# Attention with experts: biases turned group by group behind the first scores, and logits with the values' weights stationary

## The chip, the cores and the metric

One core of a Trainium2 chip. TensorE (PE) multiplies, VectorE (DVE), ScalarE (ACT) and GpSimd (POOL) do elementwise work, SyncE issues most transfers. The metric is the device time of one launch in microseconds; the kernel before takes 784.1 us, the median of 3 runs (784.02 to 784.55). All arithmetic is in fp32. A layer named tile records the kernel's operations and adds the waits between engines; an engine works through its operations in the order in which the kernel names them.

## The reference

Attention over 8 batches of 8 heads, 576 positions, 64 channels, with a bias made of a running sum; its output, 512 channels per token, goes to one of 8 experts per token.

```
# attention, per batch and head
scores = q @ k.T / 8
cum    = cumsum(max(s, 0))                       # one number per position
bias   = min(-(cum[i] - cum[j]), 0)
attn   = softmax(where(j > i, -1e9, scores + bias))
x      = attn @ v                                # (B, S, H * D) after the heads are put side by side
# experts, per token
logits     = x @ w_gate                          # 8 numbers
local_gate = sigmoid(x @ w_local)                # 1 number
e   = argmax(logits) if first token or local_gate < 0.5 else the expert of the token before
out = softmax(logits)[e] * (relu(x @ w1[e]) @ w2[e])
```

## The kernel before

Two heads make a pair; there are 32 pairs (`NPAIR`). The 576 positions are four blocks of 128 keys (`NF`) and a tail of 64 (`TL`); queries stand in nine tops of 64. A pair's scores are computed key by key (keys in partitions) in three units, each in a two-bank PSUM buffer of a pool of three; ScalarE makes weights of them with `exp(scale * score + bias)`, where the bias is one number per key, relative to the middle of one of two groups of queries (`GROUPS`). So the running sum has to be turned once, at the start, from heads in partitions to keys in partitions:

```
spin(18)                                          # 18 matmuls of the identity, results unused
nc.vector.tensor_scalar_max(s_sb, s_sb, 0.0)
cum = t_in.tile([BH, S], F32, name="cum")
nc.vector.tensor_tensor_scan(cum, ones, s_sb, 0.0, op0=Alu.mult, op1=Alu.add)

bps = ps_s.tile([P, 2, 512], F32, name="bps", tag="s")[:, 0]
bias_of, at = {}, 0
for g, (q0, q1) in enumerate(GROUPS):
    n = -(-q1 // P) * P if g == 0 else S
    rel = t_in.tile([BH, n], F32, name=f"rel{g}")
    nc.vector.tensor_scalar(rel, cum[:, :n], cum[:, MIDS[g] : MIDS[g] + 1], None, Alu.subtract)
    for c, a in enumerate(range(0, TS, P)):
        if a + P <= n:
            tr(bps[:, at : at + BH], rel[:, a : a + P], ident[:BH, :BH])      # 3 in group 0, 4 in group 1
            ...
for h in range(2):
    mm(bps[h * TL : h * TL + TL, at : at + NPAIR], lhsT=rel[:, TS:], rhs=ident[:BH, h:BH:2], start=True, stop=True)
...
nc.vector.tensor_copy(bias, bps[:, :at])
```

Two PSUM banks, `banks[0]` and `banks[1]`, take the rows: weights times values, for two sets of query tops. The values' tile holds, beside the values of both heads, a column of ones for the sums, and room for the token's logits: `v @ [w_gate, w_local]` is computed ahead and set beside `v`, so that the rows come out with the token's share of the logits. Before, the small weights are stationary in four column groups (32 columns each, 18 of them in use), the values stream, and the result is turned in VectorE:

```
scores_of_tail = banks[0][:, 3 * VW : 3 * VW + TL]                  # VW = 148
gates = banks[1][:, 2 * VW : 2 * VW + NB * SLOT].rearrange("p (c n) -> p c n", c=NB)   # SLOT = 32, NB = 5

def tail_scores(n):
    for h in range(2):
        d = slice(DH * h, DH * h + DH)
        mm(scores_of_tail[d], lhsT=ins[n][1][:, TS:][:, d], rhs=ins[n][0][:, TS:], start=True, stop=True)

def gate_parts(n):
    m = P // 4
    v = ins[n][2].rearrange("p (c n) -> p c n", c=NB)
    for j in range(0, P, m):
        mm(gates[j : j + m], lhsT=wz[:, n % HP], rhs=v[:, :, j : j + m], start=True, stop=True)

def beside_v(n):
    nc.vector.transpose(ins[n][3][:, :, 1 + DH : 1 + DH + SLOT], gates)
```

The rows of a pair, and the loop over pairs:

```
for h, d in enumerate(PARTS):                     # inside rows(n, g), for each query top i
    out = y[:, h * VW // 2 : (h + 1) * VW // 2]
    last = i * TL == TS
    if last:
        todo[half].append((out, scs[n, "tail"], v[:, NF, d], True, False))
    for c in cs:
        ...
        todo[half].append((out, scs[n, u][:, h, at : at + TL], v[:, c, d], not last and c == 0, c == cs[-1]))

tail_scores(0)
for n in range(NPAIR + 1):
    load(n + 3)
    if n < NPAIR:
        for u, pieces in enumerate((((0, 0), (3, 1)), ((0, 1), (1, 1)), ((2, 0), (2, 1), (1, 0)))):
            scores(n, u)
            for piece in pieces:
                weights(n, piece)
                if piece == (0, 0):
                    tail(n)                       # ScalarE reads the tail's scores
            ...
        seen_tail(n)
    ...                                           # steps of the sorting of tokens by expert
    if n:
        rows(n - 1, 1)
        divide(n - 1, 1)
        rows(n - 1, 0)
    else:
        spin(8)
    if n + 1 < NPAIR:
        tail_scores(n + 1)
    if n:
        divide(n - 1, 0)
    if n < NPAIR:
        gate_parts(n)
        beside_v(n)
    ...
```

In the experts' part, two of the gathered blocks of tokens are turned on PE (`product`, `x` is 128 tokens by their channels):

```
for c in range(DK):                               # DK = 4
    for h in range(2):
        self.nc.tensor.matmul(ps[h * DH : h * DH + DH, c, :], lhsT=rows[:, c, X0[h] : X0[h] + DH], rhs=self.ident,
                              start=True, stop=True)
```

## Time and profile before

| what | value |
|---|---|
| time, median of 3 runs | 784.1 us |
| span of the profiled execution | 782.4 us |
| VectorE, ScalarE, GpSimd busy | 43%, 30%, 23% |
| attention, first to last rows | 17.9 to 241.5 us |
| moved by transfers | 205.56 MB, 263 GB/s on average |

Line numbers (L406) are those of the kernel before. In a group of the profile, `o<-v,sc 128*64 128x74 f32 x3072` names the tiles written and read, the used rows and columns of the array (128 rows, 64 columns of weights), the streamed operand (128 partitions, 74 columns), and the number of records; an fp32 matmul leaves two records. Two numbers follow: busy time in us and the mean duration of one in ns, and then how long the engine was idle ahead of them. PE is the multiplying, PEld the loading of weights. Durations of records overlap, so the pace of PE is the distance between the starts of its records.

### The profile page before, as it was taken

The page shows a single profiled execution, that of the slowest core. Times are in us where ns is not written, and L with a number is a line of the kernel's source. Part 1 is how long each engine was busy: PE and PEld are TensorE (multiplying, and loading weights), DVE is VectorE, ACT ScalarE, POOL GpSimd, SP SyncE. Part 2 cuts the span into 40 slices and gives each one's busy share as a digit, 9 for nine tenths or more (in the row PEclk, how much of TensorE's full clock was granted, in tenths as well). Part 3 has the DMA queues.
Part 4 walks back from the last instruction along what each step waited for, and adds up shares of the span by engine and source line. Part 5 has one row for each costly group of instructions (what it writes and reads, how often), then busy time and mean ns, then how long its engine had stood idle before and what let it go on. Part 6 is the DMA issues. An engine that isn't in the chain of part 4 may idle for free.

```text
span 782.4 us, 17629 instructions
## 1 busy us (share of the span) xinstructions
PE 773.0 (99%) x6782; PEld 546.2 (70%) x6782; DVE 339.0 (43%) x1196; ACT 237.2 (30%) x611; POOL 176.2 (23%) x329
## 2 busy tenths in 40 slices
PE   9999999999999999999999999999999999999996
PEld 8888888888887846836677366773657736676762
DVE  2334444455566748315562156521565215635000
ACT  5777767776762111111111111111111111111110
POOL 4432345456450421011110111101111011011001
PEclk9999999999999999999999999999999999999999
DMA  9586679988655499966997569976699766994001
GB/s 314 187 300 194 201 244 327 326 285 262 210 208 217 131 354 390 409 228 221 376 395 297 199 224 380 392 290 208 233 365 389 297 211 228 368 409 175 10 13 44
DMA packets 64141, 205.56 MB, mean 263 GB/s; under 512 B 8269, under 2 KB 8301, under 8 KB 64048
## 3 DMA queue, kind: packets, MB, share of 16 engines
q1 hardware_dynamic: 55008, 173.55, 62.3%
q0 software_dynamic: 8896, 30.47, 10.4%
q8 instruction: 55, 0.90, 0.5%
q10 hardware_dynamic: 144, 0.33, 0.1%
q14 instruction: 38, 0.31, 0.1%
HBM read 181.08 MB, written 23.76 MB: 262 GB/s over the span
## 4 chain that ended last, share of the span: by engine, by line
issue 58%; PE 32%; POOL 5%; DVE 2%; POOLq 2%; DMA 1%; DVEq 0%
PE o L406 14%; PE ps L335 11%; POOL out_dram L1261 2%; POOL xg L1196 2%; PE hp L1243 2%; PE o L374 2%; PE o L291 1%; POOLq L1171 1%; DMA x_rows<-x,r_slot_i 1%; PE o L356 1%; PE bank L956 0%; DVE xT L1097 0%; POOL x_rows L1047 0%; PE bank L1107 0%; PE bank L981 0%
## 5 line engine op out<-in xcount | busy, mean ns | idle before, releaser
L1097 DVE STREAM_TRANSPOSE xT<-xg 32x128 f32<-32x128 f32 x576 | 174.1, 302 | 174.2 <-PE hp L1243 92.7
L1256 PE MATMUL yp<-w,hT 128*128 128x512 f32 (+1 forms) x528 | 216.4, 593 | 0.0
L1243 PE MATMUL hp<-xT,w 128*128 128x256 f32 (+1 forms) x1088 | 192.3, 337 | 0.3 <-DVE xT L1097 0.3
L1243 PEld LDWEIGHTS hp<-xT,w 128*128 128x128 f32 x1088 | 172.1, 191 | 24.6 <-issue 8.2
L344 ACT ACTIVATE sc<-ps,bias 128x256 f32<-128x256 f32 (+3 forms) x448 | 156.5, 482 | 53.6 <-PE ps L335 51.2
L1256 PEld LDWEIGHTS yp<-w,hT 128*128 128x128 f32 (+1 forms) x528 | 90.1, 180 | 114.6 <-issue 113.3
L1261 POOL DMA_INDIRECT out_dram<-y,at_gate x38 | 38.5, 1013 | 433.9 <-ACT y L1260 419.0
L406 PE MATMUL o<-v,sc 128*64 128x74 f32 x3072 | 113.6, 228 | 0.8 <-issue 0.8
L406 PEld LDWEIGHTS o<-v,sc 128*64 128x64 f32 x3072 | 108.8, 136 | 8.1 <-issue 4.3
L1247 ACT ACTIVATE hT<-hp 128x512 f32<-128x512 f32 x68 | 40.6, 597 | 193.0 <-PE hp L1243 193.0
L1260 ACT ACTIVATE y<-yp,at_gate 128x512 f32<-128x512 f32 x38 | 26.1, 687 | 239.8 <-PE yp L1256 233.6
L335 PE MATMUL ps<-q,k 64*128 64x320 f32 (+2 forms) x768 | 92.5, 386 | 0.1
L350 POOL TENSOR_SCALAR_AFFINE_SELECT sc<-sc 128x256 f32<-128x256 f32 x160 | 66.5, 420 | 115.9 <-issue 59.1
L335 PEld LDWEIGHTS ps<-q,k 64*128 64x128 f32 x768 | 68.9, 186 | 20.0 <-issue 4.8
L1256 PE MATMUL yp<-x,hT 128*128 128x512 f32 (+1 forms) x144 | 63.2, 594 | 0.0
L1234 DVE STREAM_TRANSPOSE hT<-x 32x256 f32<-32x256 f32 x64 | 27.9, 436 | 65.4 <-ACT x L1228 64.5
L1243 PEld LDWEIGHTS hp<-xT,x 128*128 128x128 f32 x320 | 46.1, 191 | 5.8 <-issue 2.6
L1243 PE MATMUL hp<-xT,x 128*128 128x128 f32 (+1 forms) x320 | 50.1, 317 | 0.0
L416 DVE RECIPROCAL recs<-o 128x4 f32<-128x4 f32 x64 | 12.1, 189 | 87.0 <-PE o L406 63.1
L1256 PEld LDWEIGHTS yp<-x,hT 128*128 128x128 f32 (+1 forms) x144 | 25.3, 178 | 26.2 <-issue 26.0
L1047 POOL DMA_INDIRECT x_rows<-x,r_slot_i x40 | 38.7, 968 | 10.1 <-issue 5.9
L419 DVE TENSOR_TENSOR x<-o,recs 128x292 f32<-128x292 f32 x64 | 34.4, 538 | 2.2
(162 smaller groups left out, 339.8 us busy)
## 6 DMA issues: line engine op xcount, KB each, us to landing
w<-in_w_dram SPq DMA_DIRECT2D x184, 512.0 KB, 9.5
x<-in_w_dram SPq DMA_DIRECT2D x56, 512.0 KB, 9.3
v<-in_vx_dram SPq DMA_DIRECT2D x32, 405.0 KB, 5.8
vt<-in_vz_dram SPq DMA_DIRECT2D x32, 320.0 KB, 3.9
k<-in_kz_dram SPq DMA_DIRECT2D x31, 320.0 KB, 5.1
q<-in_q_dram SPq DMA_DIRECT2D x32, 288.0 KB, 5.4
xg<-x_rows POOLq DMA_DIRECT2D x30, 293.0 KB, 8.5
x_rows<-r_empty SPq DMA_DIRECT2D x6, 293.0 KB, 3.6
```

The lines of the kernel that those rows point to most:

```text
L335: mm(ps[:, h, at : at + z - a], lhsT=kb[d, c * P : c * P + P], rhs=qb[d, a:z], start=True, stop=True)
L344: nc.scalar.activation(scs[n, u][:, h, at : at + z - a], raw[u][:, h, at : at + z - a], Act.Exp, bias=bias[:, i : i + 1], scale=scale)
L350: nc.gpsimd.affine_select(out=x, in_=x, compare_op=Alu.is_ge, fill=0.0, base=0, pattern=[[0, 2], [1, P]], channel_multiplier=-1)
L406: mm(y, lhsT=w, rhs=x, start=start, stop=stop)
L419: nc.vector.tensor_tensor(x, y, rec.unsqueeze(3).to_broadcast([P, t1 - t0, 2, HW]), op=Alu.mult)
L1047: self.s.nc.gpsimd.indirect_dma_start(out=next(self.s.views)[:, :], out_offset=bass.IndirectOffsetOnAxis(ap=self.slot[:z, m : m + 1], axis=0),
L1097: self.nc.vector.transpose(self.xT[i][d : d + m, :, k * P + a * m : k * P + a * m + m], rows[a * m : a * m + m, :, X0[d // DH] + d % DH :] ...
L1234: nc.vector.transpose(hT[i][d : d + m, :, a : a + m], x[a : a + m, :, d : d + m])
L1243: mm(y, lhsT=w[0][:, c, f : f + P], rhs=xT[i][:, c, :], start=(c == 0), stop=(c == DK - 1))
L1247: nc.scalar.activation(hT[i][:, g : g + per], ps, Act.Relu)
L1256: mm(ps[n * m : n * m + m, :], lhsT=hT[i][:, c, a : a + m], rhs=wn[:, c, :], start=(c == 0), stop=(c == FK - 1))
L1261: nc.gpsimd.indirect_dma_start(out=next(outs)[:, :], out_offset=bass.IndirectOffsetOnAxis(ap=at[i, k][:, 0:1], axis=0), in_=y[:, :], eleme ...
```

## The change

It has two parts. One is at the start: the spinning is shorter, the first pair's tail scores and two of its three score units come ahead of the biases' turning, the second group's subtraction is on GpSimd, and each group is turned into a bank of its own and copied by itself. The other takes back a layout: the values are stationary again in the logits' matmuls (64 columns at a time) and the small weights stream, so no turning in VectorE is needed, but two copies. With that the 18 columns need no slot of 32, a token's row is logits, values, values, logits, its 128 values lie side by side, the tail's rows of both heads are one matmul, the PE turning of tokens is a plain transpose, the tail's scores move to `banks[1]`, and each division follows its rows. The purpose of the first part is a shorter start, that of the second a simpler layout.

```diff
-SLOT = 32
-VX = 2 * DH + SLOT + 2
-PARTS = slice(0, VW // 2), slice(VX - VW // 2, VX)
-X0 = 0, 2 * HW - DH
+X0 = E + 1
...
-    scores_of_tail = banks[0][:, 3 * VW : 3 * VW + TL]
-    gates = banks[1][:, 2 * VW : 2 * VW + NB * SLOT].rearrange("p (c n) -> p c n", c=NB)
+    TAIL = 2 * VW
+    GATE = TAIL + TL
...
-    spin(18)
+    spin(11)
     nc.vector.tensor_scalar_max(s_sb, s_sb, 0.0)
     cum = t_in.tile([BH, S], F32, name="cum")
     nc.vector.tensor_tensor_scan(cum, ones, s_sb, 0.0, op0=Alu.mult, op1=Alu.add)
-    bps = ps_s.tile([P, 2, 512], F32, name="bps", tag="s")[:, 0]
+    bps = ps_s.tile([P, 2, 512], F32, name="bps", tag="s")
+
+    tail_scores(0)
+    for u in range(2):
+        scores(0, u)
...
-        nc.vector.tensor_scalar(rel, cum[:, :n], cum[:, MIDS[g] : MIDS[g] + 1], None, Alu.subtract)
+        (nc.gpsimd if g else nc.vector).tensor_scalar(rel, cum[:, :n], cum[:, MIDS[g] : MIDS[g] + 1], 1.0,
+                                                      Alu.subtract, Alu.mult)
...
-                tr(bps[:, at : at + BH], rel[:, a : a + P], ident[:BH, :BH])
+                tr(bps[:, g, width[g] : width[g] + BH], rel[:, a : a + P], ident[:BH, :BH])
...
-    nc.vector.tensor_copy(bias, bps[:, :at])
+    for g in range(2):
+        nc.vector.tensor_copy(bias[:, width[0] * g :][:, : width[g]], bps[:, g, : width[g]])
...
-            mm(scores_of_tail[d], lhsT=ins[n][1][:, TS:][:, d], rhs=ins[n][0][:, TS:], start=True, stop=True)
+            mm(banks[1][d, TAIL : TAIL + TL], lhsT=ins[n][1][:, TS:][:, d], rhs=ins[n][0][:, TS:], start=True, stop=True)
...
+    gates = banks[1][:, GATE : GATE + NB * 2 * (E + 1)].rearrange("p (c h e) -> p c h e", c=NB, h=2)
     def gate_parts(n):
-        m = P // 4
-        v = ins[n][2].rearrange("p (c n) -> p c n", c=NB)
-        for j in range(0, P, m):
-            mm(gates[j : j + m], lhsT=wz[:, n % HP], rhs=v[:, :, j : j + m], start=True, stop=True)
+        m = P // 2
+        for c in range(NB):
+            for j in range(0, P, m):
+                mm(gates[j : j + m, c], lhsT=ins[n][2][:, c * P + j : c * P + j + m], rhs=wz[:, n % HP],
+                   start=True, stop=True)
 
     def beside_v(n):
-        nc.vector.transpose(ins[n][3][:, :, 1 + DH : 1 + DH + SLOT], gates)
+        v = ins[n][3]
+        nc.vector.tensor_copy(v[:, :, 1 : E + 2], gates[:, :, 0])
+        nc.vector.tensor_copy(v[:, :, VW - E - 2 : VW - 1], gates[:, :, 1])
...
+                if last:
+                    todo[half].append((y, scs[n, "tail"], v[:, NF], True, False))
...
             rows(n - 1, 1)
-            divide(n - 1, 1)
             rows(n - 1, 0)
...                                                (the division now stands at the end of rows)
-                scores(n, u)
+                if n or u == 2:
+                    scores(n, u)
...
         for c in range(DK):
-            for h in range(2):
-                self.nc.tensor.matmul(ps[h * DH : h * DH + DH, c, :], lhsT=rows[:, c, X0[h] : X0[h] + DH], rhs=self.ident,
-                                      start=True, stop=True)
+            self.nc.tensor.transpose(ps[:, c, :], x[:, 2 * c * HW + X0 : 2 * c * HW + X0 + P], self.ident)
```

## Prediction

> **What bounds the kernel now.** I read the page first: busy shares, then the chain, then the groups of the lines that the change touches.

> ```profile
> PE 773.0 (99%) x6782; PEld 546.2 (70%) x6782; DVE 339.0 (43%) x1196; ACT 237.2 (30%) x611; POOL 176.2 (23%) x329
> ```

> PE is never idle for long; the other engines are under half busy. PE's busy time contains overlap, so I don't take it as a limit by itself, but the records leave only four holes above 80 ns: 1.55 us at the start, 0.13 us at 101, 0.84 us at 237 and 0.34 us at 241. So what PE gains or loses in its own order is gained or lost by the kernel, with one exception: at 237 PE waits for the last pair's weights.

> Next the chain in order of time, for its first 30 us (start, duration, what):

> ```profile
> 1.55 7.06 PE o L291 x36
> 8.62 0.58 PE bps L307 x7
> 9.19 0.23 PE bps L312 x4
> 9.43 0.27 PE o L356 x4
> 9.69 2.79 PE ps L335 x24
> 12.48 1.98 PE o L291 x16
> 14.46 0.27 PE o L356 x4
> 14.73 0.41 PE o L374 x8
> 15.14 2.79 PE ps L335 x24
> 17.93 3.42 PE o L406 x99
> ...
> 21.52 0.41 PE o L374 x8
> 21.93 2.79 PE ps L335 x24
> 24.72 3.42 PE o L406 x99
> ```

> The chain is PE alone. One pair of heads costs 24.72 - 17.93 = 6.79 us: scores (L335) 2.79, rows (L406) 3.4, tail scores (L356) 0.2, logits (L374) 0.41. There are 32 pairs. At the front stand 36 records (18 matmuls) of spinning, then the biases' turning, then the first scores.

> Third, the groups by shape:

> ```profile
> L406 PE MATMUL o<-v,sc 128*64 128x74 f32 x3072 | 113.6, 228 | 0.8 <-issue 0.8
> L406 PEld LDWEIGHTS o<-v,sc 128*64 128x64 f32 x3072 | 108.8, 136 | 8.1 <-issue 4.3 <-DVE tail L366 2.9 <-DVE r_code L944 0.5
> L374 PE MATMUL o<-vt,wz 128*32 128x160 f32 x256 | 15.7, 311 | 0.0
> L374 PEld LDWEIGHTS o<-vt,wz 128*32 128x32 f32 x256 | 5.1, 108 | 2.2
> ```

> Each fp32 matmul has two records: 256 are 4 matmuls for 32 pairs, 3072 are 48. A weight load takes 108 ns for 32 columns, 136 for 64, 191 for 128 (L1243): 0.87 ns per column on top of some 80 ns that overlap.

> [...] Two records in different column halves start 6 ns apart, and from the last tail-score pair (64 columns, halves) to the first logits record (quarters) pass 152 ns, where streaming 64 columns takes 56. So a change of mode costs about 96 ns. [...] my 0.87 ns per column gives 56. [...] Here spin records start every 213 ns up to 7.4 us and every 112 ns after.

> **The logits, 31 pairs that count** (the last pair's lie in front of the hole at 237).
> Before: from the first tail-score record to the next scores 21.12 to 21.86 = 0.74 us, with the switch from halves to quarters in it. Two passes of 160 columns: 0.16 us from the first to the second, 0.23 from there to the scores.
> After: 10 matmuls, 20 records, as 10 concurrent pairs (two halves), each with 64 columns of weights and only 18 to stream. They have the tiling of the rows and tail scores, so the first switch goes: the tail scores shrink from 0.33 to 0.23. What is the pace of a pair? In L406 it is 64 ns, where 74 columns at 0.83 to 0.84 ns (320 columns of L335 take 269) make 62: streaming bounds it, and two loads in parallel fit inside. With 18 columns streaming is 15 ns, so the load bounds: 56 plus a few, I choose 60. 9 x 60 = 0.54, then 0.015 for the last stream and 0.1 for the switch to the scores' 64 rows. Sum 0.23 + 0.54 + 0.115 = 0.89 us against 0.74: +0.155 per pair, x 31 = **+4.8 us**.

> **The tail's rows.** Two matmuls of 74 columns become one of 148: one load fewer, the same streaming, on the half of the array that was no shorter than the other. 0.

> **DVE.** One turning of 342 ns becomes two copies of 45 elements. The bias copy (480 elements 657 ns) and the reciprocal (4 elements 183) give about 1 ns per element: some 225 ns each, +0.1 us per pair. Their reader, the rows, comes 3 us later on PE: off the path.

> **A new tie through one PSUM bank.** Tail scores now lie in the bank of the first rows. In the program as built, the first rows matmul waits for ScalarE's tail weights of the next pair. In the trace before, that ScalarE instruction ends 0.40 us ahead of the rows' first record in most pairs (24.25 against 24.65), but only 0.00 to 0.14 ahead in eight of the 30, where the sorting work had kept ScalarE. Those eight may lose 0.05 to 0.1 each: **+0.5 us**. The tail scores now wait for VectorE's division of the first rows, which ends 0.265 us earlier in the first sixteen pairs: nothing.

> **The front.** Seven spins fewer: 22 records end at 6.40 instead of 36 at 8.5. The first q's last packet lands at 6.02, in time. Tail scores and two of the three score units cost 0.3 + 0.94 + 0.84 at full clock[...], +0.5: until 9.0. The turnings take 0.8 as before: last result at about 10.0 (SBUF subtraction on GpSimd is done by then; GpSimd is free from 6.6 us). Though the copies are split, in the built program the first of them waits for the last turning of the second group. So 10.05 + 0.3 + 0.45 = 10.8, and the third score unit, which needs the buffer of both, waits for both: PE stands for about 0.9 us. It runs 10.9 to 11.8, and the eight spins behind it start 0.6 us earlier than before (12.4). ScalarE starts 0.4 us earlier than its 10.86, which is worth nothing while PE leads. I take **-0.5 us**.

> **Two PE turnings of tokens** (L1107), 1.02 us each on the chain at 250.45 and 255.92, as eight matmuls of half width: 109 ns a pair. Now four full-width transposes with a single record each (those of the biases have one): 4 x 0.11, and no switch from and to the experts' full tiling, 2 x 0.1. About 0.5 saved each: **-1.0 us**.

> Sum: 4.8 + 0.5 - 0.5 - 1.0 = +3.8; 784.1 + 3.8 = **787.9 us**.

> **Rivals.**
> (a) The loads of two halves don't run in parallel when streaming no longer hides them: 2 x 56 = 112 ns a pair, +0.62 us per pair, +19 us in all: 803, slower by 2.4%. Against it: L406 sustains 64 ns a pair with the same loads. A floor of 79 ns, which two records of 2 columns in the sort (L981) show, would make +0.33 per pair: 793.
> (b) The pace falls to 50 or less, and the removed switch pays for the extra matmuls: +0.06 per pair, 785.
> (c) The tie through the bank acts in every pair: ScalarE's tail becomes the end of the wait, some 0.3 us each: 797. Against it: 0.40 us of room in 22 of 30 pairs[...].
> (d) The front gains more, because ScalarE led rather than PE: up to 2 us less, 786. Against it: the chain shows no ScalarE there, and ScalarE's wait of 8 us ended with PE's scores.

> **Range and chances.** The pace between 50 and 80 ns gives -3 to +6 around the centre, the front and the tie +-1 each. Range 785.3 to 793.0. To be faster by 2% 15 us would have to go, and nothing removed is that large; to be slower by 2% needs (a) in full.

> **What would show it.** Right: ten pairs of logits records 55 to 65 ns apart, 6.95 us from one pair's rows to the next, no ScalarE hole on PE above 0.15 us, an idle PE of about 1 us near 10 us, and product stages of 0.5 us. Wrong: a pace above 80, or PE waits on the tail weights in most pairs.

## The result, and the profile after

The changed kernel takes **790.7 us** (790.22 to 791.25, 4 runs), the kernel before beside it 784.06 (783.42 to 784.55): ratio **1.0085**, 95% interval 1.0068 to 1.0103. The prediction was 787.9 with a range of 785.3 to 793.0. The direction, the range and the cost of the new logits held; about 5 us of the measured sum come from something that no term of the prediction had, and some of it was given back elsewhere. The range had been set for the pace of the logits, the front and the tie; that it held this as well is luck.

The busy shares on the page of the changed kernel:

```profile
PE 775.8 (98%) x7064; PEld 558.1 (71%) x7064; DVE 337.9 (43%) x1228; ACT 237.3 (30%) x611; POOL 178.1 (23%) x330
```

PE has 282 more matmul records and only 2.8 us more busy time, although its last record ends 6.8 us later (782.6 in place of 775.8). So a good part of the difference is PE standing, not PE working.

The chain in order of time (start, duration, what), first 30 us:

```profile
7.03 2.44 POOL rel L324
...
10.26 0.73 DVE bias L338 x2
...
11.13 1.13 PE ps L301 x8
...
17.84 3.41 PE o L416 x95
...
21.44 0.55 PE o L378 x19
21.98 2.79 PE ps L301 x24
24.77 3.42 PE o L416 x95
```

Two things are to be seen. From rows (L416) to rows is 24.77 - 17.84 = 6.93 us, where it was 6.79: logits (L378) 0.55 in place of 0.41. And at the front the chain is no longer PE alone: it runs through GpSimd's subtraction (L324) and VectorE's bias copies (L338).

The groups by shape that answer to those of before:

```profile
L378 PE MATMUL o<-wz,vt 128*64 128x18 f32 x640 | 25.5, 209 | 1.0 <-issue 1.0
L378 PEld LDWEIGHTS o<-wz,vt 128*64 128x64 f32 x640 | 23.2, 137 | 1.2 <-issue 1.2
```

The mean of 209 ns is the length of one record, which overlaps its neighbours, and not the pace; from one pair of logits records to the next it is 58 to 59 ns. The idle time at L378 (last column) was 0.0 before; it has "issue" now, and PE's list of waits between 14 and 250 us shows the same (us in total, times, longest):

```profile
PE o L416 <- issue: 1.8, 3, 0.9
PE o L378 <- issue: 1.0, 2, 0.5
PE ps L301 <- issue: 0.9, 1, 0.9
```

"issue" means that PE waited for nothing that the profile shows. In the kernel before this list had one such stop, 0.8 us in front of the last pair's rows; one of the three at L416 here is its counterpart, at 246. The other five are new. One of them in the timeline of PE (start, length, what, count, and in brackets the idle time ahead):

```profile
138.25 1.13 PE L301 MATMUL ps<-q,k 64*128 64x256 f32 x6
140.32 1.13 PE L301 MATMUL ps<-q,k 64*128 64x320 f32 x6 [0.93 <-issue]
```

It lies in the middle of a pair's scores; the others lie within rows and logits. The profile shows no tile or buffer that becomes ready there.

**Where the 6.77 us on PE come from.** The start of the first row matmul in each of 31 pairs splits the difference of the two traces:

| stretch | predicted | measured |
|---|---|---|
| front, to the first rows | -0.5 | -0.09 (17.86 to 17.77) |
| logits, each pair | +0.155 x 31 = +4.8 | +0.134 x 30 = +4.0 |
| tie through the bank, pairs with sorting | +0.5 | +0.11 in four pairs = +0.45 |
| waits for the sort's ranks, pairs with sorting | not in the sum | -0.28 in four pairs = -1.1 |
| stops with "issue" | not in the sum | pair 17 +2.82, 18 +0.73, 19 +0.48, 28 +0.80, two small ones +0.17 = +5.0 |
| last rows to first product | 0 | -0.12 |
| turnings of tokens, first product to second | -1.0 | -1.38 |
| the rest, to the last record | 0 | 0.00 |
| sum | +3.8 | +6.8 |

### The profile page after: what moved, and what is told of

Same layout as the page of the kernel before. It is cut to its first block, busy times and chain, and to the rows that moved or that the text cites. A ratio compares the mean times of both kernels' runs of the same rounds, so it can differ in the third digit from the quotient of the medians.

```text
span 789.6 us, 18206 instructions
## 1 busy us (share of the span) xinstructions
PE 775.8 (98%) x7064; PEld 558.1 (71%) x7064; DVE 337.9 (43%) x1228; ACT 237.3 (30%) x611; POOL 178.1 (23%) x330
## 4 chain that ended last, share of the span: by engine, by line
issue 56%; PE 31%; POOL 5%; DMA 3%; DVE 3%; POOLq 1%; DVEq 0%
PE o L416 14%; PE ps L301 11%; POOL out_dram L1257 2%; PE o L378 2%; PE hp L1239 2%; POOL xg L1192 2%; DMA xg<-x_rows 1%; DVE xT L1096 1%; DMA x_rows<-x,r_slot_i 1%; POOLq L1167 1%; PE o L307 1%; PE bank L955 1%; DMA s_sb<-in_s_dram 1%; POOL x_rows L1046 0%; POOL rel L324 0%
## 5 line engine op out<-in xcount | busy, mean ns | idle before, releaser
L416 PE MATMUL o<-v,sc 128*64 128x74 f32 x3072 | 114.1, 229 | 1.8 <-issue 1.8
L416 PEld LDWEIGHTS o<-v,sc 128*64 128x64 f32 x3072 | 109.0, 136 | 9.1 <-issue 7.5
L1243 ACT ACTIVATE hT<-hp 128x512 f32<-128x512 f32 x68 | 40.6, 597 | 191.9 <-PE hp L1239 191.9
```

What stands on the lines that cost most here:

```text
L416: mm(y, lhsT=w, rhs=x, start=start, stop=stop)
L1243: nc.scalar.activation(hT[i][:, g : g + per], ps, Act.Relu)
```

## The experiments

They ran on other chips than the first comparison; there the kernel before takes 796.5 to 796.8 us (in its trace the pairs are 8.5 us longer, with stops of about 0.35 us in the rows of some later pairs, and the stretch from first to second product 3.2 us longer). So every ratio is to the kernel before on the same chip. The first four runs were on one chip, all later ones on another. Stages are compared with the trace of the kernel before on the second chip; there is none from the first, but the kernel's medians on the two agree within 0.4 us. "First rows" is the start of the first row matmul, "pairs" the 30 intervals from there to the last.

**Theory A**: the new logits cost 0.134 us in each pair, and PE's "issue" stops are for its own program: a 16 KB block of instructions that lands late. **Theory B**: the stops are waits that the change made, through its buffers or its order.

What speaks for A in the trace of the changed kernel: the numbers of the PE records (loads, matmuls and the waits of PE's own sequencer counted together, from the start) at the five stops are 5057, 5313, 5569, 5825 and 8641, which is 193 modulo 256 each time. The queue named "instruction" moves packets of 16,384 bytes, which is 64 bytes for each of 256 records. PE has some 14,300 records in all, which makes 56 such blocks, and this queue has 58 packets (before: 13,750, 54 and 55).

### One part alone: the front

```diff
 # kernel before, with only the front of the change
-    spin(18)
+    spin(11)
 ...
+    tail_scores(0)
+    for u in range(2):
+        scores(0, u)
 # two subtractions on VectorE and GpSimd, turnings and copies apart
```

> The kernel before with the first part of the change alone (11 spins, first scores ahead of the turnings, second subtraction on GpSimd, two banks, two copies); logits and token layout stay as before. Read from the trace of the changed kernel, where this front brings the second pair's tail scores 0.22 us earlier: 783.8 us, the same as before, at most 0.3 less. If the front were worth what I predicted, 0.5 less. If the stops of PE at 132 to 154 us in the changed kernel come from the front (another phase of everything behind it), they stand here too and the time is 787 to 788; if they come from the layout, none here.

Measured: 798.73 us, ratio 1.0021 (1.0010 to 1.0032). The pairs sum to 223.97 us, as in the kernel before on these chips (223.81), so the front has no effect beyond the first rows. These start at 19.58, where before starts them at 17.95: +1.6. The chain shows why: GpSimd's subtraction from 7.36 to 9.80, copies until 11.33, scores until 12.59, and then the eight spins take 3.59 us in place of 1.98: the granted clock was at half from 12.70 to 16.11. That the stands of PE before it brought this about is not shown: the two traces of the changed kernel have such stands too (0.36 or 1.04 us, and 0.92) and stay at full clock. The front is not a gain, and it can be a loss.

### The other part alone: layout, logits, turnings

```diff
 # the changed kernel, with only the front of before
-    spin(11)
+    spin(18)
 # biases: two subtractions on VectorE, one copy; tail scores and scores behind them
```

> The changed kernel with the front of before (18 spins, turnings first, both subtractions on VectorE, one copy). Regular part: +0.134 us for each of 30 pairs is +4.0, the two turnings of tokens -1.4, tail of the front +0.1: +2.7. If the stops of PE belong to the layout (more PE instructions in a pair), some 3 to 4.5 us come on top: 790 to 791. If they were an accident of the phase, 787.

Measured: 801.09, ratio 1.0054 (1.0037 to 1.0070). First rows at 17.93 (before 17.95), regular pair 6.930, pairs 230.06: +6.2 against 223.81. So the pairs' loss comes with this part. By its median it is 4.3 us slower than before, between the 2.7 expected without stops and the 5.7 to 7.2 with them. Two of the stops are there as well, in other pairs: at 57.0 and 139.5 us, records 1985 and 5313, again 193 modulo 256, though this kernel has seven spins more ahead of them.

### Moving the transfers

```diff
-            at(14 + i, 0, lambda bank, i=i: load_weights(nc, w, w1, w2, EARLY[0], (i,)))
+            at(22 + i, 0, lambda bank, i=i: load_weights(nc, w, w1, w2, EARLY[0], (i,)))
```

The four stops from 132 to 154 us coincide with the experts' weights that are loaded during pairs 14 to 21; here they are loaded eight pairs later.

> The changed kernel with the eight early transfers of the first expert's weights (0.5 MB each) issued at pairs 22 to 29 in place of 14 to 21. Theory A, PE waits for its own instructions, whose transfers stand behind those weights: the four stops at 132 to 154 us go, others may come at 180 to 235; without new ones 787 us, with as many 790 to 791. Theory B, the stops are waits of the new tie through the bank or of VectorE's copies: they stay where they are, 790.5.

Measured: 804.91, ratio 1.0100 (1.0083 to 1.0117). No stop at a block's edge between 120 and 180 us; one in pair 23, in the stretch the loads were moved to, which cost that pair 3.1 us against the other traces with the new logits:

```profile
189.08 0.47 PE L378 MATMUL o<-wz,vt 128*64 128x18 f32 x11
190.78 0.47 PE L378 MATMUL o<-wz,vt 128*64 128x18 f32 x9 [1.23 <-issue]
```

It is at record 7105, 193 modulo 256 again; the block's packet ran from 188.45 to 189.34. This agrees with A, though one stop in one trace is little to show that the loads are the cause. The 3.1 us are 1.2 of stop and, from 192.56 to 195.97, a granted clock of 0.5. Nor is the whole time to be held against the later loads: the clock was at half from 11.65 to 18.48 as well, and the first rows start at 21.70 (18.67 in the changed kernel's trace on the second chip).

### Fewer instructions

```diff
-            spin(8)
+            for i in range(2):
+                mm(banks[1], lhsT=ident, rhs=ins[0][0][:, :512], start=True, stop=True)
```

> The changed kernel with the eight spins of the first round of pairs (8 matmuls of 128 columns) replaced by two of 512 columns: the same 1.7 to 1.8 us of PE, but 6 matmuls, that is 24 PE instructions, fewer in front of everything. Theory A (blocks of 256 PE instructions): stops stand again at PE record numbers that are 256 apart and at the same remainder as before (194 of 256), so 24 instructions later in the pair, on other operations; time 788 to 791, by luck. Theory B: the stops stay on the same operations of the same pairs and move by 24 in the record number.

Measured: 803.07, ratio 1.0108 (1.0064 to 1.0151), in runs from 799.5 to 809.3. The profiled run, the fastest of them, has no stop over 0.4 us at a block's edge; its pairs sum to 228.45, +4.6, which is the 4.0 of the logits and little else. The spread between its runs is as large as the effect: nothing follows for the count of instructions. One small sign for A is there: at record 5569, again 193 modulo 256 although 24 records fewer stand ahead, PE goes on 0.30 us after the record before it and 1.5 us after a packet's end.

### The kernel before and the changed kernel on one chip

Both unchanged.

> The kernel before, unchanged, run for its trace on the chip of the experiments, so that pairs are compared on one chip. Ratio 1.000 by construction. Theory A (PE stops because a 16 KB block of its own instructions arrives late behind the transfers) expects any stop of over 0.5 us in the 32 pairs at a PE record number that is about 193 modulo 256 and 1.2 to 1.6 us after the end of an instruction packet. Theory B (the stops are waits that the change created) expects none here. The regular pair: 6.796 us.

> The changed kernel, unchanged, on the same chip. Theory B (waits made by the new order) expects the four stops of 132, 139, 146 and 153 us and the one of 223 us again, in the same pairs, since the program is the same. Theory A (late instruction blocks) expects stops only at record numbers that are about 193 modulo 256, but not necessarily the same ones[...]. Ratio to before 1.008 if the stops come in like number, 1.003 if few come. Regular pair 6.930.

Measured: before 796.47, ratio 1.0003 (0.9996 to 1.0010); changed 803.51, ratio 1.0086 (1.0057 to 1.0114). The regular pair is 6.796 and 6.930. Of the five stops of the first trace two are there, at records 5569 and 5825, and three are not. The same program has them in one trace and not in the other, and each time at 193 modulo 256, so they aren't waits that its order or its buffers make: B falls. In every one, on any chip, PE goes on 1.2 to 1.6 us after the end of an instruction packet:

| kernel | PE resumes | record, mod 256 | instruction packet | after its end |
|---|---|---|---|---|
| changed, first chip | 133.16 | 5057, 193 | 130.64 to 131.56 | 1.59 |
| | 140.31 | 5313, 193 | 137.85 to 138.84 | 1.47 |
| | 146.07 | 5569, 193 | 143.62 to 144.62 | 1.45 |
| | 153.71 | 5825, 193 | 151.39 to 152.33 | 1.38 |
| | 223.70 | 8641, 193 | 221.36 to 222.46 | 1.23 |
| changed, again | 146.23 | 5569, 193 | 143.74 to 144.75 | 1.48 |
| | 155.24 | 5825, 193 | 152.82 to 153.76 | 1.47 |
| layout alone | 57.01 | 1985, 193 | 54.50 to 55.50 | 1.52 |
| | 139.51 | 5313, 193 | 135.86 to 137.98 | 1.53 |
| weights later | 190.78 | 7105, 193 | 188.45 to 189.34 | 1.43 |

The packets took 0.9 to 1.1 us but for one of 2.12, and PE waited the longer for that. Of the 37 blocks that PE enters between 20 and 250 us in the first trace of the changed kernel, none is entered sooner than 2.3 us after its packet began (but one, where the last packet is already the next block's); 25 of them have 3 to 6 us. The stops are where that distance is at its floor. Paired in their order rather than by nearness in time, packets and blocks show the same floor without the exception, in all thirteen traces of this document: of 693 blocks none is entered sooner than 2.29 us after its packet began.

In the second trace of the changed kernel the stop at 153.8 cost more than its own length. Timeline:

```profile
152.60 1.18 PE L416 MATMUL o<-v,sc 128*64 128x74 f32 x26
155.24 0.54 PE L416 MATMUL o<-v,sc 128*64 128x74 f32 x8 [1.46 <-issue]
```

and two windows behind it (length, then busy time of PE, PEld, DVE, ACT, POOL, then the granted clock, DMA share and GB/s):

```profile
158.00:160.00 2.00, 2.00 (x14) 1.71 (x12) 0.57 (x3) 0.99 (x3) 0.33 (x2) 0.50 0.72 214
160.00:162.00 2.00, 2.00 (x20) 1.44 (x18) 0.31 (x1) 2.00 (x7) 1.17 (x3) 0.73 0.94 329
```

The clock was at 1.00 from 156 to 157 and at 0.84 in the next microsecond; so it was at half from about 157.7 to 161: pair 19 took 11.26 us, some 3.4 more than in the other traces with the new logits on these chips, for a stop of 1.46. The stop of 1.23 us with the later weights was followed by half clock too; the stops of 0.9 us in the first trace were not, and neither was one of 1.41 us in a run below (copies on GpSimd, at 35.8). The half clock lasted 3.41 us each time. The 1.41 us show that the length of one stop alone does not settle whether it comes; what does is open.

### The old logits in the changed kernel

```diff
 # the changed kernel, with the logits of before
+        turned = p_gt.tile([P, NB, SLOT], F32, name="turned")
+        nc.vector.transpose(turned, gates)
+        nc.vector.tensor_copy(v[:, :, 1 : E + 2], turned[:, :, : E + 1])
+        nc.vector.tensor_copy(v[:, :, VW - E - 2 : VW - 1], turned[:, :, E + 1 : 2 * E + 2])
```

> The changed kernel with the logits of before (weights stationary, four column quarters, turned by VectorE into a scratch tile and copied beside the values), and the new front, the new layout of the tokens and the whole-width turnings kept. Theory: the new logits cost 0.134 us in each pair, so the regular pair falls back to 6.796 us and the kernel gains 31 x 0.134 = 4.2 us on the changed one, more if its instruction stops go too. Against before: the turnings give -1.4, the front between -0.1 and +1.5 on this chip: ratio 0.998 to 1.000. Rival: the cost lies in the tie through the bank or in the merged tail rows rather than in the logits; then the pair stays at 6.85 or above.

Measured: 798.95, ratio 1.0024 (1.0013 to 1.0035). The regular pair is 6.800: the 0.13 us are the logits'. (This kernel has the old tail rows, the old places of the tail scores and of the divisions, and four buffers for the gathered tokens, which the change had raised to five; but the trace puts the whole difference between the first tail-score record and the scores, 0.875 us in the changed kernel and 0.74 before, and the rows take 3.41 and 3.42.) The first rows start at 17.81 and the stretch between the products is 34.50 in place of 36.01, -1.5; in all kernels with the new layout on these chips it is 1.3 to 1.6 shorter, with four buffers for the gathered tokens (34.50 to 34.69) as with five (34.45 to 34.75). But the pairs sum to 226.32, 2.5 more than before's, nearly all of it in pairs with sorting. What PE's loads wait for (us in total, times, longest):

```profile
PEld ps L306 <- DVE r_rank L1027: 3.2, 4, 0.9
PEld ps L306 <- ACT r_v L978: 3.0, 4, 1.3
```

and in the kernel before on this chip:

```profile
PEld ps L335 <- DVE r_rank L1015: 1.9, 4, 0.5
PEld ps L335 <- ACT r_v L966: 1.0, 4, 0.5
```

VectorE now has 0.36 us of copies more in each pair (190 and 170 ns), and they stand in front of the sort's steps for which PE waits. The ratio lies above the 0.998 to 1.000 that was expected. These waits are not the whole reason: in the profiled run the clock was at half from 287.63 to 291.04, at the start of the second product, which costs 1.7 us more (half of these 3.41, an estimate). Seven of the eleven traces on these chips have such a stretch there, the kernel before's does not.

### Mending the front

```diff
 # the last kernel, with
-    bps = ps_s.tile([P, 2, 512], F32, name="bps", tag="s")
+    bps = banks[1]
-    for u in range(2):
-        scores(0, u)
+    scores(0, 0)
-        (nc.gpsimd if g else nc.vector).tensor_scalar(rel, cum[:, :n], cum[:, MIDS[g] : MIDS[g] + 1], 1.0,
-                                                      Alu.subtract, Alu.mult)
+        nc.vector.tensor_scalar(rel, cum[:, :n], cum[:, MIDS[g] : MIDS[g] + 1], None, Alu.subtract)
 # turnings, one copy of the biases, then
+    scores(0, 1)
+    scores(0, 2)
-            spin(8)
+            spin(3)
```

> As the run with the old logits, and the front mended: both subtractions on VectorE, the biases turned into the second output bank so that no score unit waits for their copy, one copy, the second and third score units behind the turnings, and 3 spins in place of 8. Expected on top of that run: the stops of 0.35 us for GpSimd and 0.9 us for the copies go, -1.2 us, and 5 spins of 224 ns, -1.1 us, if ScalarE's first weights are there in time; -2.3 in all if PE leads, about 0 if ScalarE leads there. Ratio to before 0.995 to 0.998.

Measured: **794.48**, ratio **0.9985** (0.9974 to 0.9997): faster than before, by 0.15%, and than the changed kernel, though not within the expected 0.995 to 0.998. First rows at 15.23, -2.58 against the last run and -2.72 against before. Its chain:

```profile
6.59 1.06 PE ps L306 x8
7.65 0.42 PE o L330 x7
...
8.36 0.67 DVE bias L338
...
9.12 0.33 ACT sc L354
```

Scores, turnings of both groups and the copy follow one another, and ScalarE starts at 9.12 (before on this chip 10.95).

### The mended front alone, and the copies on GpSimd

The first is the kernel before with that front and nothing else. The second is the run above with

```diff
-        nc.vector.tensor_copy(v[:, :, 1 : E + 2], turned[:, :, : E + 1])
-        nc.vector.tensor_copy(v[:, :, VW - E - 2 : VW - 1], turned[:, :, E + 1 : 2 * E + 2])
+        nc.gpsimd.tensor_copy(v[:, :, 1 : E + 2], turned[:, :, : E + 1])
+        nc.gpsimd.tensor_copy(v[:, :, VW - E - 2 : VW - 1], turned[:, :, E + 1 : 2 * E + 2])
```

> The kernel before with the mended front of the last run alone (11 spins, tail scores and first scores, both subtractions on VectorE, turnings into the second output bank, one copy, the other score units behind the turnings, 3 spins); layout, logits and turnings of the tokens as before. Theory: the front gives -2.7 us to the first rows (17.95 to 15.2), as in that run, and the pairs stay at 6.796 and 7.6 to 7.9, since VectorE's two small copies, which kept the sort's scalings back by 0.5 us and made PE wait for them, are not here: 796.5 - 2.7 = 793.8, ratio 0.9966, although the 1.4 us of the tokens' turnings is not gained. Rival: the pairs of the last run were slower because they begin 2.7 us earlier against the transfers; then they are slower here too, and the ratio is 0.9995.

> The last run with the mended front, with the two small copies beside the values moved from VectorE to GpSimd. Theory (the copies hold VectorE while the sort's chain needs it): the stops of scores for the sort's scaling on ScalarE and its ranks on VectorE go or shrink from 2.7 us in all to below 0.6, and the kernel gains about 2 us on that run, ratio 0.996; unless GpSimd's copies hold the sort's own work on GpSimd instead. Rival (the pairs are slower for their timing against the transfers): stops as they were, ratio 0.9985.

Measured: 795.86, ratio 0.9987 (0.9977 to 0.9997), and 794.91, ratio **0.9973** (0.9966 to 0.9980), the best of the ratios. By its ratio the first could be either the theory's (0.9966) or the rival's (0.9995), and the second misses its 0.996; the pairs decide.

In both, all pairs from the fourth on are those of the kernel before to within 0.15 us; pairs 12 and 20, which cost 0.34 us each more with the copies on VectorE, differ by less than 0.01. With the copies on GpSimd the two waits fall from 3.2 and 2.3 in the run above to 1.9 and 1.4, about what the kernel before has on this chip and not the 0.6 that was expected, and another comes:

```profile
PEld o L415 <- POOL v L385: 3.1, 2, 1.7
PEld ps L306 <- DVE r_rank L1024: 1.9, 4, 0.5
PEld ps L306 <- ACT r_v L975: 1.4, 4, 0.5
```

The first is the copies queued behind GpSimd's other work, twice, once in pair 3 (+1.48 us) behind the sort's set-up. So the copies' place on VectorE was the loss, as expected. But of the 2 us expected the pairs gave back 1.1 and lost 1.48 to pair 3, and by their times this kernel and the one above can't be told apart. (The profiled runs with the mended front alone and with the copies on GpSimd had the half clock at the second product, 1.7 us each; the run above had not.)

The mended front alone gained less than the 2.7 us expected. Its first rows start at 15.96, 0.7 later than in the run above, because the input of the running sum came later: VectorE starts on it at 5.57 in place of 4.74, and in all traces between 4.66 and 6.06, whatever the kernel. So part of the 2.7 us is such a chance; this front gave 2.0 to 2.7 in three traces. And pairs 1 to 3 lost 0.87 us to late instruction blocks (records 449, 705 and 961): PE went on with record 449 at 20.93, the packet having ended at 19.45.

### Both subtractions on VectorE

```diff
-        (nc.gpsimd if g else nc.vector).tensor_scalar(rel, cum[:, :n], cum[:, MIDS[g] : MIDS[g] + 1], 1.0,
+        nc.vector.tensor_scalar(rel, cum[:, :n], cum[:, MIDS[g] : MIDS[g] + 1], 1.0,
```

> The changed kernel with the second group's subtraction on VectorE again. On this chip GpSimd's 2.44 us end at 10.37, and PE stands from 9.38 to 10.41 for it. On VectorE the subtraction of 576 columns takes about 0.5 us and ends near 8.8, ahead of PE: the stop of 1.04 us goes and the first rows start 1.0 us earlier (18.67 to about 17.65). The tokens, the logits and the pairs stay as they are: regular pair 6.930; stops at record numbers 193 modulo 256 may come or go. Ratio to the changed kernel about 0.9988, 1.0073 to the kernel before.

Measured: 801.00, ratio 1.0063 (1.0028 to 1.0098). PE's timeline in the changed kernel on this chip:

```profile
9.03 0.34 PE L328 MATMUL bps<-ident,rel 64*128 64x64 f32 x3
10.41 0.46 PE L328 MATMUL bps<-ident,rel 64*128 64x64 f32 x4 [1.04 <-POOL rel L324]
...
12.02 0.54 PE L301 MATMUL ps<-q,k 64*128 64x320 f32 x2 [0.92 <-DVE bias L338]
```

and with the subtraction on VectorE:

```profile
9.24 0.59 PE L328 MATMUL bps<-ident,rel 64*128 64x64 f32 x7
...
10.98 0.54 PE L301 MATMUL ps<-q,k 64*128 64x320 f32 x2 [0.92 <-DVE bias L338]
```

The stop for GpSimd is gone, the stop for the copies stays at 0.92, and the first rows move from 18.67 to 17.63, -1.05. That settles this step by its trace; in whole times the difference to the changed kernel lies within the intervals.

## Why the prediction was right, and where it was not

**PE's order bounds the kernel.** Held: every term above was found in the order of PE's records, and nothing that only lengthened another engine counted, until it stood in front of something that PE waited for (the copies with the old logits).

**The logits, +0.155 a pair.** Held, with a slip in the sum: 0.23 + 0.54 + 0.115 is 0.885, 0.145 above 0.74 and not 0.155, so the working gives +4.5 us for 31 pairs and +3.5 in all. From the first tail-score record to the scores the trace shows 0.875 us (before 0.74). The pace is 58 to 59 ns, 60 was chosen (from an estimate of 56 for the load of 64 columns, 0.87 ns per column); the first logits record starts 0.165 us after the first tail-score record (0.23 predicted) and the scores 0.14 after the last logits record (0.115). That a change of tiling costs some 0.1 us was an estimate too, 152 ns less 56 in the trace before; the stretch from the tail scores to the logits fell by 0.16, from 0.33. Rivals (a), two loads one after the other, and (b), a pace of 50, are out. Run with the old logits the pair falls back to 6.800.

**The tail's rows, 0, and VectorE off the path.** Held; the two copies take 196 and 194 ns by their groups (225 predicted).

**The tie through the bank, +0.5.** The size held: four pairs with sorting lose 0.11 us each. Missing was a term of the other sign. What PE's loads wait for, in the changed kernel:

```profile
PEld o L416 <- ACT tail L365: 1.6, 7, 0.2
...
PEld ps L301 <- DVE r_rank L1014: 0.5, 2, 0.3
```

and before:

```profile
PEld ps L335 <- DVE r_rank L1015: 1.6, 4, 0.5
```

Before, the scores of four pairs stood for VectorE's ranks; now PE reaches them later, the wait has shrunk by 1.1 us, and these pairs are 0.28 us cheaper than the others. That the longer logits fill that wait fits both numbers, but was only argued. Rival (c), the tie in every pair, is out: it is no part of the regular pair.

**The front, -0.5.** The +0.5 us for the first scores was an estimate from the pace of the spins, whose records start every 213 ns up to 7.4 us and every 112 after. The step that failed is "SBUF subtraction on GpSimd is done by then". It takes 2.44 us, where VectorE's of the same 576 columns took 0.50 before, and PE stands from 9.16 to 9.52 for it. From "free from 6.6 us" it would have ended at about 9.04 (an estimate from these two numbers), just in time; but the running sum's input came 0.43 us later than in the trace before (VectorE starts on it at 5.09, not 4.66), and a step with 0.1 us of room could not bear it. On the other chips, where VectorE starts at 5.99 and 6.06, the stop is 1.04 and 1.36. The idle PE "for about 0.9 us" came as predicted (0.92). Together -0.09 was left. With both subtractions on VectorE the stop for GpSimd is gone; and with the copies off the scores' buffer and five spins fewer the front gains 2.0 to 2.7 us.

**The turnings, -1.0.** Held, with 4 records each where 16 stood; on the chain of the changed kernel they are

```profile
258.63 0.44 PE bank L1104 x4
...
263.32 0.59 PE bank L1104 x4
```

in place of 1.02 each, 1.01 us less. Another 0.37 us went from the stages beside them (the sixteen product records after the first take 3.46 in place of 3.65), more than the 0.1 that was estimated for each change of tiling.

**The sum.** +3.8 was predicted, +6.8 came, and the largest part of the gap is a term that was absent: late blocks of PE's own instructions, +5.0 us in the profiled run. The prediction counted what the added instructions cost to execute and not that they must be fetched. The page before had the sign of it, an instruction queue with 55 packets, and gave no cause to look: its one long stop, at 237, is at no such edge, and a stop like it stands ahead of the last pair's rows in nearly every trace.

**What stays open.** Why late blocks cost more here. Stops at such an edge with over 0.4 us from one record to the next were 5, 2, 2, 1, 1 and 0 in six traces with the new logits, and 1 in one of seven with the old. The new pair has 292 PE records for 272, so an edge comes each 6.1 us rather than 6.4; and the stops lay where weights were being loaded. The packets themselves were not late more often: between 20 and 250 us they began more than 3.4 us after PE had entered the block before theirs in 22 of 215 cases with the new logits and in 23 of 238 with the old. That PE uses up a block 0.3 us sooner would fit, but it was not separated from chance: a stop can be missing from the next trace of the same kernel.

## What to carry to other kernels

When PE runs without a gap, price a change by the pace of records in its own tiling (here 58 to 59 ns), and then ask of every helper that it moves off PE's path whether it stands ahead of something that PE waits for later: here a 2.44 us subtraction on an idle GpSimd and 0.36 us of copies on a half-idle VectorE both reached PE. Narrow matmuls also cost program (here 292 PE records a pair for 272): a stop with "issue" in the middle of a group, at record numbers (all of PE's records counted) that agree modulo 256 and some 1.5 us after an instruction packet, was here the fetch and not a wait of the kernel. Compare such traces on one chip, and by pairs, before a difference is put down to the code.
